# Last block's result tiles: additions tile by tile, stores issued by two queues, the tile in three pieces first

## The chip, the cores and the metric

The kernel runs on one core of a Trainium2 chip. The metric is the device time of one execution in microseconds, the median of several runs. The profile is of one execution. Its engines are TensorE (PE, and PEld for its weight loads), VectorE (DVE), ScalarE (ACT), GpSimd (POOL) and SyncE (SP). DMAs are issued from the instruction streams of SP and ACT (SPq and ACTq in the profile), and the transfers themselves are carried out by 16 DMA engines.

## The reference

A retention layer (linear attention with a decay for each head) is followed by a gated feed-forward layer. Inputs and output are float32.

```python
B, H, S, D_ = 8, 8, 576, 64
scores = (1 / np.sqrt(D_)) * np.matmul(q, k.transpose(0, 1, 3, 2))
gamma = 1.0 - 2.0 ** (-5.0 - np.arange(H))
rel = pos[:, None] - pos[None, :]
Dmat = np.where(rel >= 0, gamma[:, None, None] ** rel[None, :, :], 0.0)
attn_out = np.matmul(scores * Dmat, v)

x = attn_out.transpose(0, 2, 1, 3).reshape(B * S, H * D_)    # 4608 x 512
gate = 1.0 / (1.0 + np.exp(-(x @ w_gate)))                   # w_gate: 512 x 1536
val = x @ w_val                                              # w_val: 512 x 1536
out = gate * val @ w_out                                     # w_out: 1536 x 512
```

The result has 4608 rows (tokens) of 512 columns, 9.44 MB.

## The kernel before

The tokens are worked on in columns of a transposed x: first a block of 512, then the blocks of `BLOCKS` (256, 384, 384 and then 512 each). Six blocks have 512 columns in this list, starting at 1536, 2048, 2560, 3072, 3584 and 4096; the last one, at 4096, is called the last block here. While the feed-forward layer of one block runs on TensorE, the retention steps of later tokens are woven in, until all are done. In the last block nothing is woven in any more: the profile shows TensorE with feed-forward work alone.

For a block, `h_units` makes gate and value for 12 chunks of the 1536 hidden columns (matmuls at L790, the sigmoid on ACT at L814, the product on DVE at L818) into tiles `gv`. Then, for blocks of 512, `quarters` computes the product with `w_out`. It takes the block as two halves of the tokens (even rows and odd rows of the result), and the 512 result columns as two halves of W = 256. Instead of eight block products it makes seven, numbered 1 to 7 in `OF`, from sums of `gv` tiles (`gsum`) and sums of weights (`wt_sb`), in the manner of Strassen. `product(i, ps, first)` issues the matmuls of one of them (L893), 12 matmuls into a PSUM bank: two banks are held for it, `a` and `e` (tiles qa and qe). `keep` copies a bank to SBUF on ACT (L905, tiles s1, s4, s16 and s5 for the sums of products).

The result of a block is four tiles `obs[0]` to `obs[3]` of 128 rows by 512 columns. `obs[0]` and `obs[1]` are the even rows, `obs[2]` and `obs[3]` the odd ones. `add(b, c, ps, name)` writes half c (columns 0 to 255 or 256 to 511) of tile b: one addition of a PSUM bank and a kept sum on DVE (L910, 128x256). `add_half(h, c, ps, name)` does it for both tiles of a half of the tokens. So each tile needs two additions before it is whole.

`places(b)` says where the rows of tile b lie in the result: every second row of one stretch or more. In the last block tiles 0 and 2 lie in one piece (result rows 4160 to 4415), and tiles 1 and 3 in three pieces of 32, 32 and 64 partitions (rows from 3968, 4544 and 4416). Each piece needs a DMA of its own.

In the order of the last block before the change: product 7 ends bank `a`, and four additions make tiles 2 and 3 whole, first the left half of both (L938), then the right half (L939). `stored` puts both tiles on a list, from which `leave` (L825 to L827) issues the DMAs on SP (`nc.sync`) at the next steps of the main loop: one DMA for tile 2, three for tile 3. Product 3 ends bank `e`, and two additions make the right halves of tiles 0 and 1 (L944), which `send(b, 1, nc.sync)` issues on SP: one DMA and three. At last product 2, not in `product` but for each tile by itself into a bank of its own (tile qf, six matmuls of 128x256 at L954), first tile 0, then tile 1; after each an addition of its left half (L956), and `send(b, 0, ...)` with ACT's queue for tile 0 (one DMA) and SP's for tile 1 (three DMAs). That makes twelve DMAs, eleven of them on SP, issued in the order of the program on each queue.

The other blocks of 512 share the lines up to product 3. Their tiles go through `stored`, which holds nine tiles back (`KEEP = 9`) before `leave` issues the oldest.

Of the kernel before, what the change touches and what calls it, by code (L numbers as in the profile page):

```python
# [16 lines left out]
def kernel(  # L17
# [19 lines left out]
    nc = tc.nc  # L37

    B, H, S, D = q.shape
    NT, DM = out.shape  # L40
# [68 lines left out]
    def rows(col, n):  # L109

        out_ = []
        for c0 in sorted(rows_of):
            for r0, w in rows_of[c0]:
                lo, hi = max(c0, col), min(c0 + w, col + n)
                if lo < hi:
                    x = (lo - col, r0 + lo - c0, hi - lo)
                    if out_ and out_[-1][1] + out_[-1][2] == x[1]:
                        out_[-1] = (out_[-1][0], out_[-1][1], out_[-1][2] + x[2])
                    else:
                        out_.append(x)  # L120
        return out_
# [703 lines left out]
    def leave():  # L825
        for at, to in zip(*stores.pop(0)):
            nc.sync.dma_start(out[to, :], at)  # L827
# [7 lines left out]
    def stored(ob, places):  # L835

        stores.append(([ob[at] for at, _ in places], [to for _, to in places]))
        if len(stores) > KEEP:
            leave()
# [20 lines left out]
    def quarters(gvs, sums, t0, k):  # L860

        W = DM // 2
        n = k * P
        final = t0 + 2 * n == NT

        def raw(o, h):
            return lambda fp: gvs[2 * fp + o][:, h * n:(h + 1) * n]

        def summed(i):
            return lambda fp: sums[fp][:, i]  # L870

        def plain(o, c):
            return lambda fp: wo_sb[:, 2 * fp + o, c * W:(c + 1) * W]

        def mixed(i):
            return lambda fp: wt_sb[:, i, fp]

        OF = {1: (raw(0, 0), plain(0, 0)), 2: (raw(1, 0), plain(1, 0)), 3: (summed(3), plain(1, 1)),
              4: (raw(1, 1), mixed(3)), 5: (summed(0), mixed(0)), 6: (summed(1), mixed(1)), 7: (summed(2), mixed(2))}

        def bank(name, pool=ffn_psum, tag="ffn", m=k):
            return pool.tile([P, m, W], FP32, tag=tag, name=f"q{name}_{t0}")

        def held_bank(name):
            ps = bank(name)
            ffn_psum.held.append(ffn_psum.last)
            return ps

        def product(i, ps, first):
            left, right = OF[i]  # L890
            for fp in range(NFC // 2):
                for b in range(k):
                    nc.tensor.matmul(ps[:, b], lhsT=left(fp)[:, b * P:(b + 1) * P], rhs=right(fp),  # L893
                                     start=(first and fp == 0 and b == 0), stop=(fp == NFC // 2 - 1 and b == k - 1),
                                     skip_group_check=True)
                if k > 1 and fp == NFC // 4 - 1:
                    yield k * W * NFC // 4

        tail = W * (k * NFC // 2 - (k * NFC // 4 if k > 1 else 0))
        kept = {}  # L900
        obs = {}

        def keep(name, ps):
            kept[name] = sum_pool.tile([P, 2, W], FP32, tag="sum", name=f"s{name}_{t0}")[:, 0:k]
            nc.scalar.copy(out=kept[name], in_=ps)  # L905

        def add(b, c, ps, name):
            if b not in obs:
                obs[b] = osb_pool.tile([P, DM], FP32, tag="osb", name=f"ob_{t0 + b * P}")
            nc.vector.tensor_tensor(out=obs[b][:, c * W:(c + 1) * W], in0=ps, in1=kept[name][:, b % k], op=ALU.add)  # L910

        def add_half(h, c, ps, name):
            for b in range(k):
                add(h * k + b, c, ps[:, b], name)

        def places(b):
            r = b // k
            return [(slice(p0 // 2, (p0 + w) // 2), slice(at + r, at + w, 2)) for p0, at, w in rows(t0 + b % k * 2 * P, 2 * P)]

        def send(b, c, queue):  # L920
            for at, to in places(b):
                queue.dma_start(out[to, c * W:(c + 1) * W], obs[b][at, c * W:(c + 1) * W])

        a, e = held_bank("a"), held_bank("e")
        yield from product(1, a, True)
        keep("1", a)
        yield tail
        yield from product(4, e, True)
        keep("4", e)
        yield tail  # L930
        yield from product(6, a, False)
        keep("16", a)
        yield tail
        yield from product(5, e, True)
        keep("5", e)
        yield tail
        yield from product(7, a, False)
        add_half(1, 0, a, "4")  # L938
        add_half(1, 1, a, "5")  # L939
        for b in range(k, 2 * k):  # L940
            stored(obs[b], places(b))
        yield tail
        yield from product(3, e, False)
        add_half(0, 1, e, "16")  # L944
        if final:
            for b in range(k):
                send(b, 1, nc.sync)
        yield tail
        if final:
            left, right = OF[2]  # L950
            for b in range(k):
                ps = bank(f"f{b}", *VALS[b], 1)[:, 0]
                for fp in range(NFC // 2):
                    nc.tensor.matmul(ps, lhsT=left(fp)[:, b * P:(b + 1) * P], rhs=right(fp),  # L954
                                     start=(fp == 0), stop=(fp == NFC // 2 - 1))
                add(b, 0, ps, "1")  # L956
                send(b, 0, (nc.scalar, nc.sync)[b])
                yield W * NFC // 2
            return
        g = bank("g", *VALS[0])  # L960
        yield from product(2, g, True)
        add_half(0, 0, g, "1")
        for b in range(k):
            stored(obs[b], places(b))
        ffn_psum.order = ffn_psum.held + [x for x in ffn_psum.order if x not in ffn_psum.held]
        ffn_psum.held = []
        yield tail
# [12 lines left out]
    def ffn_units(t0, n):  # L980
        gvs = {}
        sums = []
        for i, cols in enumerate(h_units(gvs, range(NFC), t0, 0, n)):
            if i % 4 == 3 and n == 512:
                sums.append(gv_sums(gvs, len(sums), 256))
            yield cols
        yield from quarters(gvs, sums, t0, 2) if sums else op_units(gvs, t0, n)
# [223 lines left out]
    for w, (t0, n) in enumerate(BLOCKS):  # L1211
# [8 lines left out]
        at = end  # L1220
        while not twos and valued + (end - begin) < last or twos and twos[-1][0][-1] < last:
            vals = list(range((twos[-1][0][-1] if twos else valued + end - begin) + 1, at))
            twos.append((vals, list(range(at, min(at + 2, NS)))))
            at = min(at + 2, NS)
# [56 lines left out]
```

## Time and profile before

| what | value |
|---|---|
| median of 3 runs | 324.52 us (324.05, 324.52, 325.1) |
| the profiled execution's own time | 324.37 us |
| its span, first to last instruction | 322.65 us (shown as 322.7) |
| granted TensorE clock | 0.996 |
| PE busy | 313.6 us, 97% of the span |
| DVE, ACT, POOL busy | 196.5, 141.5 and 139.7 us |
| DMA over the span | 55.18 MB, mean 171 GB/s |
| DMA, 314 to 322.7 us | 1.05 MB in 960 packets, 121 GB/s |
| addition at L910 on qa, 128x256 | 0.41 us each |
| issue of a store at L922 on SP | 0.39 to 0.53 us, median 0.47 |
| issue of a store at L827 on SP, from 314.5 us | 0.34 to 0.47 us, median 0.40 |
| these stores, from the start of the issue to landing | 1.6 to 2.5 us, median 1.9 |

The profile's page divides the span into 40 slices of some 8 us. In all of them but the first and the last TensorE is busy for nine tenths or more:

```profile
PE   8999999999999999999999999999999999999991
```

The part that the change touches lies in the last slice, from about 313 us on. Of the page's sums over the span little is to be learned there; the views to read are the timeline of the last 10 us, the waits of SP's queue, the issues of DMAs with their landing, and short windows of DMA share. A landing is the time from the start of the issuing instruction to the signal of the DMA's end.

### The profile page before, as it was taken

The page shows a single profiled execution, that of the slowest core. Times are in us where ns is not written, and L with a number is a line of the kernel's source. Part 1 is how long each engine was busy: PE and PEld are TensorE (multiplying, and loading weights), DVE is VectorE, ACT ScalarE, POOL GpSimd, SP SyncE. Part 2 cuts the span into 40 slices and gives each one's busy share as a digit, 9 for nine tenths or more (in the row PEclk, how much of TensorE's full clock was granted, in tenths as well). Part 3 has the DMA queues.
Part 4 walks back from the last instruction along what each step waited for, and adds up shares of the span by engine and source line. Part 5 has one row for each costly group of instructions (what it writes and reads, how often), then busy time and mean ns, then how long its engine had stood idle before and what let it go on. Part 6 is the DMA issues. An engine that isn't in the chain of part 4 may idle for free. (4 is left out here: it accounts for less than half of the span.)

```text
span 322.7 us, 9424 instructions
## 1 busy us (share of the span) xinstructions
PE 313.6 (97%) x3822; PEld 190.9 (59%) x3822; DVE 196.5 (61%) x486; ACT 141.5 (44%) x315; POOL 139.7 (43%) x192
## 2 busy tenths in 40 slices
PE   8999999999999999999999999999999999999991
PEld 7664557856546554458545864486448644864481
DVE  6855566666508864656756676647655766456622
ACT  5855545554524344337332733364335433423320
POOL 5774538442564652219521962197119111301130
PEclk9999999999999999999999999999999999999998
DMA  7999999978999999703996299419941670040004
GB/s 216 337 382 386 344 285 224 200 154 150 222 214 198 246 236 227 177 0 78 164 264 154 58 226 281 93 44 210 161 144 37 198 260 0 5 130 2 1 2 130
DMA packets 146220, 55.18 MB, mean 171 GB/s; under 512 B 125440, under 2 KB 138240, under 8 KB 146176
## 3 DMA queue, kind: packets, MB, share of 16 engines
q1 hardware_dynamic: 145488, 54.18, 69.7%
q8 instruction: 30, 0.49, 0.6%
q10 hardware_dynamic: 688, 0.39, 0.4%
q14 instruction: 14, 0.11, 0.1%
HBM read 37.75 MB, written 9.44 MB: 146 GB/s over the span
## 5 line engine op out<-in xcount | busy, mean ns | idle before, releaser
L790 PE MATMUL h<-xT,wv_sb 128*128 128x512 bf16 (+2 forms) x432 | 100.7, 356 | 0.0
L790 PE MATMUL h<-xT,wg_sb 128*128 128x512 bf16 (+2 forms) x432 | 100.7, 355 | 0.0
L814 ACT ACTIVATE g<-h 128x512 bf16<-128x512 f32 (+1 forms) x96 | 54.7, 570 | 99.6 <-PE h L790 95.5
L818 DVE TENSOR_TENSOR gv<-g,h 128x512 bf16<-128x512 bf16 (+1 forms) x96 | 62.7, 654 | 50.6 <-PE h L790 47.7
L790 PEld LDWEIGHTS <-wv_sb 128*128 128x128 bf16 x432 | 42.0, 98 | 40.4
L790 PEld LDWEIGHTS <-wg_sb 128*128 128x128 bf16 x432 | 42.0, 98 | 40.1 <-issue 0.2
L849 POOL TENSOR_TENSOR gsum<-gv 128x256 bf16<-128x256 bf16 x36 | 24.1, 668 | 87.3 <-DVE gv L818 87.3
L343 POOL TENSOR_TENSOR qk<-k,ktab 128x512 bf16<-128x512 f32 x30 | 31.4, 1048 | 24.9 <-DMA k<-in_k_dram 24.7
L343 POOL TENSOR_TENSOR qk<-q,qtab 128x512 bf16<-128x512 f32 x28 | 29.6, 1058 | 2.4 <-DMA q<-in_q_dram 2.4
L588 DVE TENSOR_TENSOR pt<-row,tri 128x256 bf16<-128x256 f32 x60 | 21.6, 416 | 13.6 <-PE row L581 12.1
L893 PEld LDWEIGHTS <-gsum 128*128 128x128 bf16 x288 | 27.7, 98 | 3.4
L348 POOL CAST v<-v 128x512 bf16<-128x512 f32 x29 | 18.4, 634 | 8.3 <-DMA v<-in_v_dram 2.9
L973 PE MATMUL op<-wo_sb,gv 128*128 128x512 bf16 x96 | 21.7, 379 | 0.0
L893 PEld LDWEIGHTS <-gv 128*128 128x128 bf16 x204 | 19.5, 98 | 3.7
L549 ACT CAST sb<-s 128x256 bf16<-128x256 f32 x44 | 16.8, 414 | 6.6 <-DVE s L702 5.7
L657 ACT CAST xT<-val 128x256 bf16<-128x256 f32 x46 | 14.5, 383 | 9.6 <-PE val L615 6.6
L893 PE MATMUL qa<-wt_sb,gsum 128*128 128x256 bf16 x144 | 17.7, 273 | 0.0
L702 DVE TENSOR_TENSOR s<-s,row 128x256 f32<-128x256 f32 x39 | 16.2, 415 | 0.8
L853 POOL TENSOR_TENSOR gsum<-gv,gv 128x256 bf16<-128x256 bf16 x6 | 4.0, 667 | 27.4 <-DVE gv L818 27.4
L973 PEld LDWEIGHTS <-gv 128*128 128x128 bf16 x96 | 9.2, 98 | 10.3
L643 DVE COPY glance<-val 128x1 f32<-128x1 f32 x24 | 2.8, 154 | 18.8 <-PE val L615 17.7
L910 DVE TENSOR_TENSOR ob<-qa,s 128x256 f32<-128x256 f32 x24 | 8.5, 414 | 7.7 <-PE qa L893 5.8
(128 smaller groups left out, 392.0 us busy)
## 6 DMA issues: line engine op xcount, KB each, us to landing
k<-in_k_dram SPq DMA_DIRECT2D x26, 256.0 KB, 3.9
q<-in_q_dram SPq DMA_DIRECT2D x26, 256.0 KB, 4.1
v<-in_v_dram SPq DMA_DIRECT2D x26, 256.0 KB, 4.5
out_dram<-ob SPq DMA_DIRECT2D x25, 256.0 KB, 2.8
wg<-in_moe_w_gate_dram SPq DMA_DIRECT2D x12, 256.0 KB, 5.1
wv<-in_moe_w_val_dram SPq DMA_DIRECT2D x12, 256.0 KB, 5.1
wo<-in_moe_w_out_dram SPq DMA_DIRECT2D x12, 256.0 KB, 4.7
v32p<-in_v_dram SPq DMA_DIRECT2D x6, 256.0 KB, 4.4
```

The costliest lines, as they stand in the source:

```text
L343: eng.tensor_tensor(out=natural_qk[s][:, i].rearrange("p m (y d) -> p y m d", y=2), in0=by_halves(loaded[s][1 - i]), in1=tab, op=ALU.mult)
L348: eng(out=natural["v", s], in_=loaded[s][2])
L549: eng(out=state[key], in_=src)
L588: nc.vector.tensor_tensor(out=probs[s][:, y], in0=row_ps[s][y][:, 0], in1=tri.unsqueeze(1).to_broadcast([P, M, 64]), op=ALU.mult)
L657: nc.scalar.copy(out=x_out(ALL, cols_of(s, i)), in_=x_in(val_ps[s][i], cols_of(s, i)))
L702: nc.vector.tensor_tensor(out=new, in0=running[b], in1=p, op=ALU.add)
L790: nc.tensor.matmul(out, lhsT=w_sb[:, kc, fc * P:(fc + 1) * P], rhs=xT(kc, slice(t0 + a, t0 + e)), start=(kc == 0), stop=(kc == NKC - 1))
L814: nc.scalar.activation(out=g[:, 0:n], in_=h1[:, 0:n], func=AF.Sigmoid)
L818: nc.vector.tensor_tensor(out=gvs[some[0]][:, a:e], in0=g[:, 0:n], in1=h2[:, 0:n], op=ALU.mult)
L849: nc.gpsimd.tensor_tensor(out=t[:, 2], in0=a11, in1=a21, op=ALU.subtract)
L893: nc.tensor.matmul(ps[:, b], lhsT=left(fp)[:, b * P:(b + 1) * P], rhs=right(fp), start=(first and fp == 0 and b == 0), stop=(fp == NFC // ...
L973: nc.tensor.matmul(opp, lhsT=gvs[fc][:, nb * P:(nb + 1) * P], rhs=wo_sb[:, fc, :], start=(fc == 0), stop=(fc == NFC - 1))
```

## The change

In all blocks of 512 the four additions after product 7 are made tile by tile: left and right half of tile 2, then left and right half of tile 3, each tile given to `stored` when it is whole.

In the last block, tiles 2 and 3 are no longer put on the list of `stored`; `send` issues their DMAs at once. `send` takes a range of columns, and gives its DMAs to SP and ACT in turn: each DMA issued reverses the list of the two queues, across tiles too. After product 3 the right half of tile 0 alone is sent (one DMA); that of tile 1 stays back. The last product takes tile 1 first and tile 0 second. Tile 1 is then sent whole, all 512 columns in three DMAs, and of tile 0 the left half. That makes nine DMAs: on SP tile 2, a piece of 32 of tile 3, the right half of tile 0, a piece of 32 of tile 1 and the left half of tile 0; on ACT a piece of 32 and the one of 64 of tile 3, and the same of tile 1.

```diff
-        def send(b, c, queue):
+        queues = [nc.sync, nc.scalar]
+
+        def send(b, c0=0, c1=DM):
             for at, to in places(b):
-                queue.dma_start(out[to, c * W:(c + 1) * W], obs[b][at, c * W:(c + 1) * W])
+                queues[0].dma_start(out[to, c0:c1], obs[b][at, c0:c1])
+                queues.reverse()
...
         yield from product(7, a, False)
-        add_half(1, 0, a, "4")
-        add_half(1, 1, a, "5")
-        for b in range(k, 2 * k):
-            stored(obs[b], places(b))
+        for b in range(k):
+            add(k + b, 0, a[:, b], "4")
+            add(k + b, 1, a[:, b], "5")
+            if final:
+                send(k + b)
+            else:
+                stored(obs[k + b], places(k + b))
         yield tail
         yield from product(3, e, False)
         add_half(0, 1, e, "16")
         if final:
-            for b in range(k):
-                send(b, 1, nc.sync)
+            send(0, W, DM)
         yield tail
         if final:
             left, right = OF[2]
-            for b in range(k):
+            for b in reversed(range(k)):
                 ps = bank(f"f{b}", *VALS[b], 1)[:, 0]
                 for fp in range(NFC // 2):
                     nc.tensor.matmul(ps, lhsT=left(fp)[:, b * P:(b + 1) * P], rhs=right(fp),
                                      start=(fp == 0), stop=(fp == NFC // 2 - 1))
                 add(b, 0, ps, "1")
-                send(b, 0, (nc.scalar, nc.sync)[b])
+                send(b, 0, DM if b else W)
                 yield W * NFC // 2
             return
```

## The prediction

> **What bounds the kernel now.** I read first the chain of work that ended last, since the change touches only the way in which result tiles leave. Its end, in the stretch from 290 us:
>
> ```profile
> 313.33 1.31 PE qe L893 x12
> 314.64 1.32 PE qf L954 x12
> 315.96 0.03 issue
> 315.99 0.42 DVE ob L910
> ```
>
> TensorE sets the pace up to 315.96, one addition on VectorE follows, and the chain stops at 316.41. The span is 322.65 us. So 6.24 us lie behind the last computation, and the chain does not tell of them, because it holds no transfers. The timeline of the last stretch does (start, duration, engine, line, operation; SPq and ACTq are the issuing of DMAs by SP and ACT):
>
> ```profile
> 313.17 1.47 PE L893 MATMUL qe<-wo_sb,gsum 128*128 128x256 bf16 x12
> 313.42 1.42 DVE L910 TENSOR_TENSOR ob<-qa,s 128x256 f32<-128x256 f32 x4 [5.85 <-PE qa L893]
> ...
> 314.48 1.47 PE L954 MATMUL qf<-wo_sb,gv 128*128 128x256 bf16 x12
> 314.54 1.81 SPq L827 DMA_DIRECT2D out_dram<-ob  x4
> 314.76 0.74 DVE L910 TENSOR_TENSOR ob<-qe,s 128x256 f32<-128x256 f32 x2
> 315.42 0.41 DVE L910 TENSOR_TENSOR ob<-qf,s 128x256 f32<-128x256 f32 x1
> 315.86 0.39 ACTq L922 DMA_DIRECT2D out_dram<-ob  x1
> 315.99 0.42 DVE L910 TENSOR_TENSOR ob<-qf,s 128x256 f32<-128x256 f32 x1 [0.16 <-PE qf L954]
> 316.44 3.63 SPq L922 DMA_DIRECT2D out_dram<-ob  x7
> ```
>
> SP issues eleven stores without a break from 314.54 to 320.08, 5.54 us or 0.50 us each. The first of the seven at L922 has its data from 315.17 on (the first of the two L910 additions that began at 314.76) and begins only at 316.44, when the four of L827 are out of the way. ACT issues one store and is idle otherwise. What lies behind the last issue:
>
> ```profile
> SPq L827 <- DVE ob L910: 26.9, 2, 26.7
> SPq L1276 <- DMA out_dram<-ob: 1.5, 1, 1.5
> ```
> ```profile
> 319.61 0.47 SPq L922 DMA_DIRECT2D out_dram<-ob  x1
> ```
>
> The waits of SP say that after 320.08 it waited once, 1.5 us, for a store; then the program closes. The last store was issued at 319.61 and, by the view of DMA issues for that moment, landed 1.9 us later, at 321.51. From there to the end of the span are 1.14 us. So the end is: last issue 319.61 + landing 1.9 + closing 1.14 = 322.65.
>
> Is it the issuing, or the data? The windows after the last computation:
>
> ```profile
> core 0: us, PE busy (x) PEld busy (x) DVE busy (x) ACT busy (x) POOL busy (x), PEclk, DMA share, GB/s
> 306.40:316.50 10.10, 9.55 (x86) 8.21 (x84) 3.52 (x9) 2.49 (x5) 2.59 (x4) 1.00 0.11 37
> 316.50:321.60 5.10, 0.00 (x0) 0.00 (x0) 0.00 (x0) 0.00 (x0) 0.00 (x0) 0.86 0.48 135
> ```
>
> With all engines idle, the DMA engines are busy for 0.48 of the time and move 135 GB/s; in 315.50 to 316.00 they moved 401. They wait for issues, so SP's issuing bounds the last stretch.
>
> **The change part by part.**
>
> Fewer issues. Tile 1 (rows in pieces of 32, 32 and 64 partitions) went out in halves, 3 + 3 issues; now once, whole, 3 issues. The last block goes from 12 stores to 9, with the same 1.05 MB: at 0.50 us each, 1.5 us less issuing.
>
> Two queues. The order of the built program gives SP five issues (tile 2 whole; a piece of 32 of tile 3; right half of tile 0; a piece of 32 of tile 1; left half of tile 0) and ACT four (32 and 64 of tile 3, 32 and 64 of tile 1). Ahead of them ACT has only its four copies to s, done at 312.64; nothing is queued behind, so waits of ACT's issues hold up nobody else. The row of ACT's issue (315.86, 0.39 us) beside SP's at 315.87 (0.47 us) shows both issuing at once.
>
> Additions tile by tile. The four additions on qa begin about 0.34 us apart (313.42 to 314.43). Before, tile 2 was complete with the third, at 314.50; now with the second, at 313.76 + 0.41 = 314.17, 0.33 us earlier; tile 3 stays at 314.84. The other blocks take the new order too: I cost this at nothing, since SP's order of stores in them is unchanged, TensorE's bank is free after the same fourth addition, and their stores are kept back for several tiles. If the cover were gone, a block would lose at most one addition's step, 0.34 us, in five blocks 1.7 us; I take 0, as DVE is idle 39% of the span and PE's order is untouched.
>
> The three-piece tile first in the last product. The six matmuls of tile 1 now end where those of tile 0 did, and its addition takes the slot of 315.42 to 315.83; tile 0's takes 315.99 to 316.41. Same work, no cost; both banks have long been idle.
>
> The new schedule, from these rows: SP issues tile 2 at 314.21; ACT and SP tile 3's first pieces at 314.88; ACT its 64 at 315.27; SP the right half of tile 0 at 315.3, done by 315.8; both tile 1's pieces of 32 at 315.86; ACT its piece of 64 at 316.25 (to 316.33, were its issue as long as SP's); SP the last, the left half of tile 0, at 316.44, just after its data. The issue that sets the end starts at 316.44 in place of 319.61: 3.17 us earlier.
>
> A new wait: ACT's last issue waits for the semaphore of tile 2's store. That one took 2.0 us to land, so it is through at 314.21 + 2.0 = 316.21, ahead of 316.25: 0. Bounds: with the longest landing of the last stretch, 2.5 us, it would be 316.71, and 0.46 us late for that store alone.
>
> The landing of the last store was 1.9 us for 64 KB on nearly idle DMA engines; now it is 128 KB in the thick of others. Bounds: 1.6 us (the shortest store, 32 KB) and 2.5 us (the piece of 64 of tile 3, issued beside another). I take 2.2: the store of the same form (128x256, 128 KB), which was issued at 316.44 too, 0.6 us after 256 KB of others, as in the new schedule. ACT's last, 316.25 + 1.9 to 2.5, is within 0.2 us of it.
>
> Can the data keep up? In 314 to 322.7 the two queues' packets took 35.5% and 4.3% of 16 engines, 3.46 us of all of them, for 1.05 MB, half of it in 1 KB packets. The first data moved at about 315.4 (share 0 up to 315.25, 0.45 in the quarter after it), and with tile 2 issued 0.33 us earlier move at 315.1. From there 3.46 us end at 318.5, if nothing gets dearer; a landing at 316.44 + 2.2 = 318.64 goes with that.
>
> The Trainium skill speaks against a gain here: "DMA: Bandwidth & Descriptors", section "Issuing engines are not separate DMA queues", says that starting DMAs from several engines saves only the sequencer's time to start them, which is usually small beside the DMA. By its word "usually small" the sum would be near nothing, and the time 324.5 us. Here the row decides otherwise: 5.54 us of issuing against 3.46 us of moving.
>
> Sum: 316.44 + 2.2 + 1.14 = 319.78 against 322.65, so 2.87 us less. The profiled execution took 324.37 us with this span (1.72 around it); the median of the three runs is 324.52, 0.15 above. 324.52 - 2.87 = 321.65, **321.7 us**. With landings of 1.6 and 2.5, the latter with the late wait (316.71 + 2.5, in place of 318.64), it is 321.05 and 322.2.
>
> **The rivals.**
>
> (1) The queues take turns: issues of SP and ACT do not run side by side when there are many. Then eight issues from 314.88 at 0.50 us end at 318.9, the last beginning at 318.4, 1.2 us ahead of 319.61; with the landing of 1.9: 323.3. Against it: the pair at 315.86. For it: SP's own issues stretched from 0.34 to 0.53 us as the DMAs piled up.
>
> (2) The DMA engines bound it. At the lowest rate of a quarter microsecond with a high share (0.80 share, 160 GB/s; full share would be 200) the data need 5.2 us from 315.1, to 320.3; before they ended at 321.2. Gain 0.9 us: 323.6.
>
> (3) The other side: stores of two queues hinder each other. Where ACT's and SP's were both out, in 316.50 to 316.75, the rate was 131 GB/s. If all of it moved so, 8.0 us from 315.1, the data end at 323.1, 1.9 us later than before: 326.4, slower. It decides only below 1.05 MB / (321.2 - 315.1) = 172 GB/s. Against it: the share was 0.45 in that quarter, so the engines were starved rather than slow, and the one ahead of them moved 401 at 1.03.
>
> (4) The change doesn't do what it says: no gain within 1 us, since something outside these rows holds the end (an instruction of ACT that comes late, say); 324.5. Nothing in the profile speaks for it; SP's last wait names a store.
>
> **How the numbers follow.** A measurement of this kernel tells about 0.3% (1 us) from no change. Forecast 0.74; (1) 0.10; (2) 0.08, which lies on the edge of that 1 us, so half of it counts as faster and half as no change; (3) 0.04; (4) 0.04. Faster is 0.74 + 0.10 + 0.04 = 0.88, same 0.04 + 0.04 = 0.08, slower 0.04. The forecast's own range is 321.05 to 322.2; runs of one kernel spread by 0.5 us to either side of the median, which takes it down to 320.9; up to 323.4 it takes in (1). Beyond that lie (2), (3) and (4), 0.16, and a little below 320.9: about 0.2 in all.
>
> **What would show it.** In the profile after: ACT issues four stores between 314.9 and 316.8 and SP five, the last at about 316.4; the last landing is 2.0 to 2.5 us after it; SP's closing wait grows from 1.5 to about 1.7 us while the span ends about 3.4 us after the last addition rather than 6.2; DMA share is over 0.8 from 315.2 to 318. Wrong, if ACT's issues start after SP's end or take over 0.6 us (1), if the share stays at 1 with under 200 GB/s (2, 3), or if chains before 313 us have moved.

## The result, and the profile after

The changed kernel took 322.03 us in the median of six runs (321.71 to 323.38), beside 324.4 us for the kernel before (324.05 to 325.1, six runs). The ratio is 0.993, with a 95% interval of 0.9909 to 0.995: faster by 0.5% to 0.9%. Forecast were 321.7 us and a gain of 2.87 us; the gain is 2.4. The profiled execution took 321.98 us, its span is 320.26 us.

The end of the timeline of the changed kernel (start, duration, engine, line, operation):

```profile
313.25 1.42 DVE L910 TENSOR_TENSOR ob<-qa,s 128x256 f32<-128x256 f32 x4 [5.85 <-PE qa L893]
314.04 2.84 SPq L924 DMA_DIRECT2D out_dram<-ob  x5
...
314.70 2.23 ACTq L924 DMA_DIRECT2D out_dram<-ob  x4
315.25 0.41 DVE L910 TENSOR_TENSOR ob<-qf,s 128x256 f32<-128x256 f32 x1
315.82 0.42 DVE L910 TENSOR_TENSOR ob<-qf,s 128x256 f32<-128x256 f32 x1 [0.15 <-PE qf L959]
```

SP issues five stores and ACT four, side by side, and both are through at 316.9. Before, SP issued until 320.08, and ACT had one store. The last addition ends at 316.24 (before: 316.41), so the rest of the span, which I call the **tail**, is 320.26 - 316.24 = 4.02 us, where it was 6.24. The tail is the better measure for what the change touches. The moment of the last addition differs by 2 us between the profiles of this study (316.07 to 318.10); three profiles of the changed kernel alone have 316.24, 317.75 and 318.10, so no edit is needed for such a difference.

The single rows of the two last issues, and what the view of DMA issues says of them (KB, us to landing):

```profile
316.46 0.47 ACTq L924 DMA_DIRECT2D out_dram<-ob  x1
```
```profile
316.50 0.38 SPq L924 DMA_DIRECT2D out_dram<-ob  x1
```
```profile
out_dram<-ob ACTq DMA_DIRECT2D x1, 128.0 KB, 2.8
out_dram<-ob SPq DMA_DIRECT2D x1, 128.0 KB, 2.9
```

Issued 3.1 us earlier than before, the last store takes 2.9 us to land where the last one before took 1.9. A part of what the earlier issue gained is given back here. (316.50 + 2.9 = 319.40; ACT's last store landed before it, at 316.46 + 2.8 = 319.26.) The windows of the stretch in which the stores move:

```profile
core 0: us, PE busy (x) PEld busy (x) DVE busy (x) ACT busy (x) POOL busy (x), PEclk, DMA share, GB/s
314.70:319.00 4.30, 1.08 (x10) 0.71 (x8) 1.39 (x4) 0.00 (x0) 0.00 (x0) 1.00 0.82 244
316.25:317.25 1.00, 0.00 (x0) 0.00 (x0) 0.00 (x0) 0.00 (x0) 0.00 (x0) 1.00 0.87 166
317.25:318.75 1.50, 0.00 (x0) 0.00 (x0) 0.00 (x0) 0.00 (x0) 0.00 (x0) 1.00 0.91 314
```

The share of the DMA engines is 0.82 from 314.70 to 319.00 (before, 0.48 behind 316.5), and 0.91 near the end. So the data now wait less for issues and more for each other. SP's closing wait goes with that, 2.3 us for stores after its last issue where it was 1.5:

```profile
SPq L1281 <- DMA out_dram<-ob: 2.3, 3, 1.2
```

### The profile page after: what moved, and what is told of

Its sections match the earlier page's. It is cut to its first block, busy times and chain, and to the rows that moved or that the text cites. A ratio compares the mean times of both kernels' runs of the same rounds, so it can differ in the third digit from the quotient of the medians.

```text
span 320.3 us, 9422 instructions
## 1 busy us (share of the span) xinstructions
PE 313.1 (98%) x3822; PEld 190.3 (59%) x3822; DVE 195.7 (61%) x486; ACT 141.3 (44%) x315; POOL 140.0 (44%) x192
```

## The experiments

Theory at first: the start of the last issue sets the end, with a landing of a little over 2 us behind it. Rival: the DMA engines bound the end, and queues and counts of issues matter little. The first four runs test parts of the change one by one, the next three and the half-bytes run ask what makes the landing long, and the last two try a faster order. All edits are against the changed kernel. In this table "last issue" is the start of the store that landed last, counted from the end of the last addition, and all columns but the median and the ratio are from the profiled execution. Each ratio is taken against runs of the kernel before made beside it; their medians were 324.4 us for the first result, 324.61 for the four parts, 324.79 for the second profile of the changed kernel and the three runs beside it, and 324.76 for the third and the last three runs. So the ratios compare better across the rows than the medians do.

| kernel | median us | ratio to before, 95% | tail us | last issue us | its landing us |
|---|---|---|---|---|---|
| before | 324.4 | | 6.24 | 3.20 | 1.9 |
| after | 322.03 | 0.9909 to 0.995 | 4.02 | 0.26 | 2.9 |
| after, second time | 322.56 | 0.9909 to 0.9945 | 3.74 | 0.11 | 2.7 |
| after, third time | 322.42 | 0.9912 to 0.996 | 4.10 | 0.27 | 3.0 |
| one queue | 323.58 | 0.9953 to 0.9979 | 5.15 | 2.02 | 2.2 |
| tile 1 in halves | 322.62 | 0.9906 to 0.9948 | 4.49 | 1.51 | 1.9 |
| tile 0 first | 322.29 | 0.9912 to 0.9956 | 4.13 | 0.41 | 2.8 |
| additions by half | 322.36 | 0.9907 to 0.9951 | 3.89 | 0.16 | 2.9 |
| whole tiles | 322.48 | 0.991 to 0.9945 | 3.56 | 0.04 | 2.5 |
| shared out by size | 322.27 | 0.9909 to 0.9941 | 3.70 | 0.35 | 2.5 |
| without tile 2 | 322.41 | 0.9908 to 0.996 | 3.64 | 0.11 | 2.7 |
| half of tiles 1 and 3 | 321.59 | 0.9891 to 0.9922 | 3.45 | 0.46 | 2.0 |
| pieces first | 322.45 | 0.9919 to 0.9946 | 3.63 | 0.04 | 2.6 |
| pieces first, one queue | 323.85 | 0.9961 to 0.999 | 4.96 | 1.88 | 2.1 |

The three profiles of the changed kernel give tails of 3.74, 4.02 and 4.10: mean 3.95, and differences of 0.2 us are not to be told apart. Every other row has one profile.

> The changed kernel once more, as the measure for the runs beside it: 321.7 to 322.4 us, span end 3.9 to 4.2 us after the last addition.

> The changed kernel once more, the measure for the runs beside it: 321.7 to 322.6 us, span end 3.7 to 4.0 us after the last addition.

### The second queue taken away

```diff
-        queues = [nc.sync, nc.scalar]
+        queues = [nc.sync, nc.sync]
```

> The changed kernel with all nine stores on SP. Theory (the start of the last issue sets the end): tile 2 at 314.0, tile 3's three from 314.7 in steps of 0.5 us, then four more, the last store issued at 318.2 where the changed kernel has 316.4; with a landing of 2.0 to 2.4 us and the closing of 0.95 to 1.14 the span ends 4.9 to 5.5 us after the last addition (before 6.24, changed kernel 4.02), time 323.0 to 323.4 us. Rival (the DMA engines bound it, two queues save nothing): 4.0 us after the last addition, 322.0 us.

The tail is 5.15 us, where the theory had 4.9 to 5.5 and the rival 4.0; the time is 323.58, 0.2 above the theory's range. The interval of its ratio lies above those of the changed kernel's first two sets of runs (up to 0.995) and meets that of the third (up to 0.996); the same edit in another order, at the end of this section, gives two intervals that lie apart. The timeline of this run and its closing wait:

```profile
314.98 4.75 SPq L924 DMA_DIRECT2D out_dram<-ob  x9
...
316.77 0.42 DVE L910 TENSOR_TENSOR ob<-qf,s 128x256 f32<-128x256 f32 x1 [0.16 <-PE qf L959]
```
```profile
SPq L1281 <- DMA out_dram<-ob: 1.5, 1, 1.5
```

SP issues until 319.74 (nine issues in 4.75 us, with 0.32 us of waiting for tile 3's data in it), 2.5 us beyond the last addition, and waits 1.5 us after its last issue, as before the change. So the second queue is worth 5.15 - 3.95 = 1.2 us of tail. What is left of the gain, 6.24 - 5.15 = 1.1 us, fits SP's eleven issues turned into nine, of which two at 0.5 us are 1.0. That is worked out, not tried: no run has twelve stores from one queue in the new order.

### Tile 1 in halves again

```diff
             send(0, W, DM)
+            send(1, W, DM)
...
-                send(b, 0, DM if b else W)
+                send(b, 0, W)
```

> The changed kernel with tile 1 in halves again, twelve stores on two queues in turn. Theory: ACT's last store, the left half of tile 0, waits behind six issues of ACT and for the semaphore of tile 3's piece of 64, which lands at 317.7: issue at 317.75, end 4.8 to 5.3 us after the last addition, 322.8 to 323.3 us; without an effect of that wait the issue starts at 317.2, 4.2 to 4.7 us after it. Rival (DMA engines bound it): data start to move earlier, 4.0 us or less, 321.7 to 322.0 us.

The last store began 1.51 us after the last addition, the tail is 4.49 us, 0.5 above the changed kernel. ACT would have been free at 317.49 + 0.54 = 318.03 and issued its last store at 318.17:

```profile
318.17 0.38 ACTq L924 DMA_DIRECT2D out_dram<-ob  x1
```

The store whose semaphore it needs, tile 3's piece of 64, was issued at 315.54 and took 2.6 us, to 318.14. These times fit the wait, at a cost of some 0.14 us; the rest of the delay is ACT's six issues. The tail came out below the range that I gave for the case with this wait (4.8 to 5.3) and within the one for no effect of it (4.2 to 4.7), since the last store landed in 1.9 us: it began 0.68 us behind the store ahead of it, and the last one before the change had taken 1.9 us too. The rival's tail of 4.0 or less did not come. So three more stores cost 0.5 us of tail where two queues issue them, less than the 1.1 us that is left for fewer stores with one queue: what a part is worth depends on the other. The median cannot be told from that of the changed kernel.

### Tile 0 first, and additions by half

```diff
-            for b in reversed(range(k)):
+            for b in range(k):
```

> The changed kernel with tile 0 ahead of tile 1 in the last product, so that the three pieces are issued last. Theory: last issue, a piece of 64, at 316.75 rather than 316.46, end 4.1 to 4.4 us after the last addition, 322.1 to 322.4 us. Rival (the order of tiles is worth as much as the second queue): 5 us or more, 323 us. Second rival (nothing): 4.0 us.

```diff
-        for b in range(k):
-            add(k + b, 0, a[:, b], "4")
-            add(k + b, 1, a[:, b], "5")
+        add_half(1, 0, a, "4")
+        add_half(1, 1, a, "5")
+        for b in range(k):
             if final:
```

> The changed kernel with the four additions after product 7 half by half again. Tile 2 is whole 0.33 us later. Theory: its store is issued at 314.4 in place of 314.04 and lands 0.33 us later; the last store of tile 0, whose semaphore is now the one that tile 2's store used, waits for that to 316.8, end 4.3 to 4.4 us after the last addition, 322.3 us. Rival (that wait and the start of the data don't matter): 4.0 us, 322.0 us.

The tail of 3.89 lies within the spread of the changed kernel and that of 4.13 is 0.03 above it, and both times lie within it. With tile 0 first the tail is also within the 4.1 to 4.4 us of the theory, so its 0.1 to 0.4 us are neither shown nor excluded. Neither the order of the last two tiles nor the order of the additions is worth anything that these runs can show. In the second the expected wait was seen (SP waited 0.3 us for tile 2's store ahead of its last issue), but SP's last issue began no later than in the changed kernel, 0.22 us after the last addition, and the rival held.

### Fewer and larger pieces

```diff
-            for at, to in places(b):
+            where = {1: [(slice(0, P), slice(4416, 4544))],
+                     3: [(slice(0, 64), slice(3968, 4032)), (slice(64, P), slice(4544, 4608))]}
+            for at, to in where.get(b) or places(b):
```

> The changed kernel with the same bytes, but tile 1's rows written to one stretch of 128 rows of the result in one store and tile 3's to two stretches of 64 rows, so the rows of these two tiles stand in another order in the output; six stores in place of nine. Theory (the last landing is long because pieces of 32 and 64 partitions move slowly and the DMA engines are busy to the end): all of the moving takes 2.7 to 3.0 us of 16 engines in place of 3.5, the last landing is 1.9 to 2.3 us in place of 2.8, the end 3.1 to 3.4 us after the last addition, 321.1 to 321.5 us. Rival (two queues in flight hinder each other, whatever the pieces): moving 3.3 us or more, the last landing 2.6 to 2.9 us, end 3.7 to 4.0 us after the last addition.

The edit also writes the rows of tiles 1 and 3 one behind the other, where `places` has every second row. The result lies between the two forecasts. The DMA queues' packets took 22.0% and 12.2% of 16 engines in 314 to 323 us, 3.08 us, where the changed kernel beside it has 21.0% and 15.3%, 3.27 us. The landing fell from 2.7 to 2.5 us, the tail to 3.56, 0.2 below the run beside it. The other two profiles of the changed kernel have 39.1% and 38.6% in the same window, 3.52 and 3.47 us, so the small pieces cost the DMA engines some 0.2 to 0.4 us, as far as one profile tells. The theory had asked for 0.5 to 0.8 us (2.7 to 3.0 in place of 3.5).

### Pieces shared out by size

```diff
-                queues[0].dma_start(out[to, c0:c1], obs[b][at, c0:c1])
-                queues.reverse()
+                queue = nc.sync if b == 2 or at.stop - at.start == 32 else nc.scalar
+                queue.dma_start(out[to, c0:c1], obs[b][at, c0:c1])
```

> The changed kernel with the pieces shared out by size: the pieces of 32 partitions and tile 2 on SP, the pieces of 64 and both halves of tile 0 on ACT, so that pieces of different partitions are in flight together and the last issue is at 0.05 us after the last addition rather than 0.25. Theory (moving bounds the end, and the slow pieces overlap better): end 3.5 to 3.9 us after the last addition, 321.5 to 321.9 us. Rival (the way in which pieces are shared out is worth nothing): 4.0 us, 322.0 us.

The tail of 3.70 is in the theory's range and 0.04 us below the run of the changed kernel beside it (3.74): nothing to be told. The last issue came 0.35 us after the last addition rather than at 0.05, as ACT's four issues took 0.53 to 0.55 us each.

### Bytes taken away, early ones and late ones

```diff
-                send(k + b)
+                if b:
+                    send(k + b)
+                else:
+                    queues.reverse()
```

> The changed kernel without the store of tile 2 in the last block: 128 rows of the output are left unwritten, 256 KB less to move ahead of the others, one issue less on SP, and no store left that waits for it. Theory (the DMA engines bound the end, each byte ahead delays the last): end 3.4 to 3.7 us after the last addition, 321.4 to 321.8 us. Rival (issue times and a fixed landing set the end; the last issues move by 0.15 us at most): 3.9 us, 321.9 us.

```diff
-                send(k + b)
+                send(k + b, 0, W if b else DM)
...
-                send(b, 0, DM if b else W)
+                send(b, 0, W)
```

> The changed kernel with tiles 1 and 3 stored in their left 256 columns alone: nine issues at the same times as before, their right halves left unwritten, 256 KB less to move, all of it in the slow pieces and half of it after the last but one addition. Theory (the moving of what becomes ready in the last microsecond sets the end): the last landing is 1.9 to 2.3 us in place of 2.6 to 2.9, end 3.1 to 3.4 us after the last addition, 321.3 to 321.6 us. Rival (the landing is long because many stores are in flight, whatever their bytes): end 3.7 to 4.0 us after it, as the changed kernel beside it.

Both leave 256 KB unmoved. (In the first, `reverse` keeps every other store on its queue.) Without tile 2, whose bytes move before most others are ready, the landing of the last store is 2.7 us and the tail 3.64. That is within the theory's 3.4 to 3.7, but only 0.1 below the run of the changed kernel beside it, so the early bytes cost little, if anything. With the same bytes taken from tiles 1 and 3, the last store lands in 2.0 us, though there are nine issues as in the changed kernel:

```profile
316.61 0.62 SPq L924 DMA_DIRECT2D out_dram<-ob  x1
```
```profile
out_dram<-ob SPq DMA_DIRECT2D x1, 128.0 KB, 2.0
```

The tail is 3.45, 0.05 above the theory's range (the time, 321.59, is within it), because SP's issues ran late and the last began 0.46 us after the last addition, not 0.26. From that issue to the end of the span are 319.60 - 316.61 = 2.99 us, where the three runs of the changed kernel have 3.63 to 3.83. This is the one run of the set that is faster than the changed kernel beside it by more than the spread, 321.59 against 322.42 us, though the two intervals meet (0.9891 to 0.9922, 0.9912 to 0.996). So with the same number of stores the landing is short again, which speaks against the rival, and for bytes that queue at the DMA engines in the last microsecond. It is one run, and the times moved with the bytes: the store ahead of the last was issued 0.47 us before it here, and 0.04 us before it in the changed kernel. How much of the 0.9 us belongs to the bytes and how much to that distance is not shown.

### Pieces first: an order meant to be faster

```diff
+        if final:
...
+            for b in reversed(range(k)):
+                half(7, a[:, b], b, False)
+                add(k + b, 0, a[:, b], "4")
+                add(k + b, 1, a[:, b], "5")
+                send(k + b)
+                yield W * NFC // 2
+                half(3, e[:, b], b, False)
+                add(b, 1, e[:, b], "16")
+                if not b:
+                    send(b, W, DM)
+                yield W * NFC // 2
+                ps = bank(f"f{b}", *VALS[b], 1)[:, 0]
+                half(2, ps, b, True)
+                add(b, 0, ps, "1")
+                send(b, 0, DM if b else W)
+                yield W * NFC // 2
+            return
```

Here `half(i, ps, b, first)` issues the six matmuls of product i for one tile. The second run of this order has all nine stores on SP (`queues = [nc.sync, nc.sync]`).

> A version meant to be faster: in the last block products 7, 3 and 2 are made for tiles 3 and 1 first (six matmuls each), then for tiles 2 and 0, so that the two tiles in pieces are whole at 2.9 and 2.0 us ahead of the last addition, and only whole tiles are left for the end. Same matmuls, additions and nine stores. Theory (slow pieces and the bytes of the last microsecond set the end): the moving starts 0.6 us earlier, the last landing is 1.9 to 2.4 us from an issue at 0.05 us after the last addition, end 2.9 to 3.4 us after it; TensorE may lose up to 0.2 us at the bank that ACT copies: 321.2 to 321.7 us. Rival (the order of tiles is worth nothing, as with tile 0 ahead of tile 1): end 3.7 to 4.0 us after it, same time as the changed kernel.

> The same version with all nine stores on SP. Theory (issues at 0.50 us bound one queue): the pieces leave from 2.9 us ahead of the last addition in steps of 0.5, SP falls behind by the fourth, and the last issue is 0.9 to 1.2 us after the last addition; end 3.8 to 4.3 us after it, 0.7 to 1.1 us slower than with two queues. Rival (with pieces out of the way early one queue is enough): within 0.3 us of the version with two queues.

A miss: 322.45 us, where the changed kernel beside it has 322.42. From the start of product 7 to the end of the last addition there are 4.72 us (312.91 to 317.63), 0.17 more than in the changed kernel beside it (313.55 to 318.10), as feared. The tail is 3.63, not 2.9 to 3.4. SP's second issue held up all behind it:

```profile
314.99 1.24 SPq L924 DMA_DIRECT2D out_dram<-ob  x1
```

With tile 3's piece of 64 stuck until 316.23, SP began tile 1's piece at 316.32 instead of 315.7 and tile 2 at 316.96, and the pieces were out of the way no earlier than whole tiles were ready. With one queue it was 1.4 us slower (323.85 us, tail 4.96), beyond the 0.7 to 1.1 us that the theory gave. SP's second issue took 1.19 us there, some 0.7 us more than the 0.5 of the forecast, and all later ones followed it without a pause. The two intervals, made beside each other, lie apart (0.9919 to 0.9946, 0.9961 to 0.999): the second queue is worth 1.3 us of tail in this order and 1.2 in the other.

## Why the prediction was right, and where it was off

**What bounds before.** Right: SP's issuing. Taking away the second queue costs 1.2 us of tail; the 1.1 us left fit two fewer issues on SP, by its rows; and undoing any other part of the change changed nothing measurable.

**Fewer issues, two queues.** Right in kind. The forecast moved the last issue from 3.20 us after the last addition to 0.03; it came at 0.26 in the profile (0.11 to 0.27 in three). The store that landed last was SP's, and it was late because SP was still issuing until 316.40: its second issue alone took 0.64 us (more on it below). The new wait, costed at nothing with a bound of 0.46 us, concerns ACT's last store, and it was up to 0.18: ACT was free at 315.75 + 0.53 = 316.28 and issued at 316.46, when tile 2's store, issued at 314.04, had landed after 2.4 us. The third profile has the same (free at 318.16, tile 2 landed at 318.30, issue at 318.35); in the second tile 2 landed before ACT was free. The view of waits does not list it, so it is read from these times alone, and in the profile shown it did not set the end.

**Additions tile by tile, order of the last product.** Costed at nothing but 0.33 us for tile 2's start; undone, they changed nothing that can be told from the spread.

**The landing.** This is the term that was mis-sized: "I take 2.2", with an upper bound of 2.5 us, against 2.9 measured (2.7 and 3.0 in the repeats). The model for it was a store that had 256 KB of others ahead of it within 0.6 us, on DMA engines that waited for issues most of the time. In the new schedule the share is 0.82, and 0.89 from 315.2 to 318.0, as the prediction's own sign (over 0.8) had it. The step "Can the data keep up?" added the moving up to 3.46 us and found that it ends at 318.5; with 3.5 us at a share of 0.82 it ended at about 318.9. It had taken the engines as full from the first byte, which they are not, and the forecast did not carry the load over to the landing of the last store, beside which ACT's of the same size was issued 0.04 us earlier. The half-bytes run, with a landing of 2.0, agrees with these bytes as the cause, with the reserve given there.

**The sum.** Against a tail of 319.78 - 316.41 = 3.37 us: issue 0.23 later, landing 0.7 longer, closing 0.86 us in place of 1.14, together 0.65, so 4.02. Luck brought the time nearer to the forecast than the mechanism: the closing (from the last landing to the end of the span) was 0.28 us shorter, for which no run gives a reason, and the last addition came 0.17 us earlier in this profile, far within the 1.9 us by which the three profiles differ. Without these two the gain in the profile would have been 1.9 us where 2.87 were forecast.

**The rivals.** Queues that take turns (1): fell, by the one-queue run and by the rows, in which an issue of ACT and one of SP overlap (315.12 to 315.65, 315.43 to 315.80). DMA engines as the bound (2): half right. With the issuing out of the way the DMA engines were busy for 0.82 and the landing grew, but at 244 GB/s, above the 200 at which the gain was to be 0.9 us. Rates fell to 166 GB/s for a microsecond at a share of 0.87, near rival (3)'s 131, but only there. Something outside these rows (4): fell, with the tail down from 6.24 to 4.02. The Trainium skill's rule, "DMA: Bandwidth & Descriptors", section "Issuing engines are not separate DMA queues", has two halves. That transfers of several queues share the same DMA engines is what the longer landing agrees with. That the issuing saved is usually small beside the transfer is not the case for these stores: in the one-queue run nine issues took 4.75 us beside 3.59 us of moving, and the second queue saved 1.2 us of a tail of 5.15.

**Open.** Why the rate was 166 GB/s at a share of 0.87 between 316.25 and 317.25. The small pieces explain some 0.2 to 0.4 us of moving; whether the two queues' packets hinder each other was not tried by itself, though with one queue all of the moving took 35.9% of 10 us, 3.59 us, no less than with two (3.27 to 3.52).

## What to carry to other kernels

The chain of work that ended last can stop well ahead of the span's end: look at the issue rows and landings behind it, and compare the time of issuing with the busy share of the DMA engines. Where a queue's issuing is the bound, as here, a second queue shortens the end, and fewer stores do by the rows; but the landing must then be priced at the DMA load of the new schedule (2.9 us), not at that of the starved profile (1.9 to 2.2). And a gain of this size is better measured from the last computation on: that moment differed by 1.9 us between three profiles of one kernel, the tail behind it by 0.4.

## What the runs showed that was not expected

The second store that SP issues in the last block (32 to 128 KB) took between 0.34 and 1.24 us to issue. In every profile in which it took over 0.6 us, one packet of 16 KB on the queue of instructions was under way, and the issue ended 0.4 us after it. In the run with pieces first the packet is alone in a window of 0.05 us from 314.70. Its share is over 100%, so its whole time is put down to the window in which it begins, and tells its length (of 16 engines):

```profile
q8 instruction: 1, 0.02, 140.8%
```

1.408 x 16 x 0.05 = 1.13 us, thus to 315.83, and the issue that began at 314.99 ended at 316.23. In the changed kernel the packet began at about 313.57 and took 1.705 x 0.8 = 1.36 us, to 314.93, and SP's second issue (314.70, 0.64 us) ended at 315.34:

```profile
q8 instruction: 1, 0.02, 170.5%
```
```profile
314.70 0.64 SPq L924 DMA_DIRECT2D out_dram<-ob  x1
```

Before the change the packet, begun at 313.8, took 1.10 us, and the issue of 314.97 took 0.38 us as others did, ending after the packet by 0.45. That SP waits there for its instructions is my inference from this coincidence; no run took the packet away, and some later issues were as long without one (0.62 and 0.63 us on SP in the half-bytes run, 0.72 us on ACT with larger pieces). If it is so, it cost the changed kernel up to 0.3 us of SP's issuing, and the faster order about 0.9.
